# Chunk C of a batch in both partition halves, its matmuls on the two row halves of the array in turn, cosine and sine transforms in successive units

## The chip, the cores and the metric

The kernel runs on one core of one Trainium2 chip. The metric is the device time of one execution in microseconds (us). The kernel before takes 688.46 us, the median of three runs (687.03 to 688.67).

The engines are named as in the profile: PE is the matmul engine, PEld its weight loads, DVE the vector engine, ACT the scalar engine, POOL the GpSimd engine, SP the engine whose queue issues nearly all DMAs here.

## The reference

The input `x` is 8 batches of 3008 rows of 256 numbers. The first half of the work is the real part of a two-dimensional Fourier transform of each batch, the second half a gated feed-forward block on every row.

```python
X = np.fft.fft(x, axis=1)
X = np.fft.fft(X, axis=2)
y = X.real.reshape(24064, 256)
g = y @ w_gate                      # 256 x 1536
h = g / (1 + exp(-g)) * (y @ w_val)  # 256 x 1536
out = h @ w_out                     # 1536 x 256
```

Inputs and output are float32. The kernel multiplies in bfloat16 and accumulates in float32.

## The kernel before, in words

**The Fourier transform.** The transform over the 256 columns is folded into the weights once (`transform_w` makes `Wp`, `Wq` and `Wm` of `w_gate` and `w_val`). What is left for each batch is the transform over its 3008 rows. Its symmetries are used up to a fold by eight: rows are added and subtracted in groups (`fold_steps`, on POOL) until 188 folded positions remain, each with an odd-row and an even-row member (index `q` = 0, 1), and with 128 columns and a remainder. The 188 positions are kept in two chunks: chunk A has 128 of them, one on each partition, and chunk C has the other 60, on the lower 64 partitions for an even batch and on the upper 64 for an odd one. So a chunk-C tile holds two batches, and one fold of it serves a pair.

`fold_steps` gives seven steps for one `q`: sums and differences `SDf` (L153, twice), the even and the odd fold over the columns (L156, L157, L160), `Af` (L163), the coefficients `CE` (L166, L167) and `BB` (L170 to L172). `CE` serves the first half of a batch's output positions (`part` 0), `BB` the second (`part` 1). 

**The transform matmuls.** `transform(b, part, eos)` multiplies these coefficients (as weights, 128 columns wide) by tables of cosines and sines `Tab` (moving). `eo` 0 is the cosine transform and ends in tile `Pt`, `eo` 1 the sine transform and ends in `Qt`. For each `q` there is one accumulator: `q` 0 in a PSUM tile `v`, `q` 1 in a PSUM tile `g`. Into each go two matmuls of chunk A (128 rows of the array), then two of chunk C (64 rows). In `part` 0 the moving side has 189 or 188 columns, in `part` 1 it has 376. The sine transform of `part` 0 has a further group, `row0` (L543): weights of one single column, for chunk A and chunk C, which fill in row 0 of the result alone. When a `q` is done, ACT copies the `v` accumulator out (`od`, L575), and DVE adds and subtracts `od` and the `g` accumulator into the tiles `Pt` or `Qt` (L580). `whole_part` calls `transform` for `eo` 0 and then for `eo` 1, at once. Batch 0 is made at the start by a longer way, in which chunk C fills all 128 rows.

**The feed-forward block.** The 12032 columns of all batches' `Pt` and `Qt` are cut into 24 tiles of up to 512 columns; each column yields two output rows (position k and its mirror image). A unit is one tile and one of the 12 blocks of 128 hidden features; there are 288. In a unit, `part_a` makes the gate `g` and the value of the first output row, and `part_b`, one unit later, those of the mirror row. In the units where `split` holds (in most tiles blocks 0, 2, 3, 5, 7 and 9), the value product is taken apart into two accumulators `e` and `o`, both from the PSUM pool of the `v` tiles; DVE makes both values of them (`es` L731, then `vv` L733 and L735), and POOL multiplies them by the gates (L736, L758). In the other units DVE does the multiplication (L744, L762). ACT does the gate function (L728, L743, L757, L761). `OWork` multiplies the finished hidden tile of the tile before by `Wo` (L676), eight matmuls in each unit. Three units' worth fill a PSUM tile `o`, which ACT copies to one of four `ev` tiles (L682), and SP sends it out (L688, two or three DMAs).

**Order.** The order on each engine is the order of the program text (a manual schedule). The loop over units runs `run_loads` (three pending loads of `x`, issued on SP), `part_a`, output work, `part_b` of the unit before, output work, the fold steps that fall due (`fold_at`, `fold_step`), and the transform that falls due (`job_at`). The transforms of a batch stand in two units, nearly all of them in block 4 of a tile, of which the next block, 5, is a split one. Where a fold's first step falls due, all its loads that are still pending are issued at once. Chunk C of batches 2 and 3 is first folded in units 25 to 44; its loads follow in SP's queue on those of chunk A of batch 1. PSUM is divided into three `v` tiles, three `g` tiles and two `o` tiles; a new tile takes the buffer that has been free in program order for longest, and its first matmul waits until that buffer's last reader is done.

The chunk-C loads of one batch (`load_c`) are 15 transfers of four positions (L137: both rows of each, 2 KB runs), 4 transfers of 60 positions for the rows counted downwards (L139), and one for the middle row (L141).

Of the kernel before, what the change touches and what calls it, by code (L numbers as in the profile page):

```python
# [31 lines left out]
def kernel(  # L32
# [8 lines left out]
    nc = tc.nc  # L41
# [57 lines left out]
    XC = const.tile([P, 8, 2, D], F32, name="XC")  # L99
    SDf = const.tile([P, 2, 4, D], F32, name="SDf")  # L100
# [31 lines left out]
    def load_c(b, q):  # L132

        X3 = XC.rearrange("p a q d -> p a (q d)")
        p0 = 64 * (b % 2)
        pm = p0 + NCR
        return ([lambda h=h: q.dma_start(out=X3[p0 + LC * h:p0 + LC * (h + 1), 0:4, :],  # L137
                                         in_=up_block(b, JC - LC * h, LC)) for h in range(NC_)] +
                [lambda a=a: q.dma_start(out=X3[p0:p0 + NCR, 4 + a, :], in_=down_set(b, a, JC, LC, NC_))  # L139
                 for a in range(4)] +  # L140
                [lambda: q.dma_start(out=XC[pm:pm + 1, 0:4, 1],  # L141
                                     in_=rows_at(b, 0, [[R * D, 1], [R * D, 4], [1, D]]))])

    def fold_steps(eng, X, CE, BB, q, r, given=None):
# [4 lines left out]
        def sd(a, op):  # L152
            tt(SDf[r, a], X[r, 0:4, q, :], X[r, 7:3:-1, 1 - q, :], op=op)  # L153
# [11 lines left out]
        def ce():  # L165
            tt(CE[r, q, :, 0, :], Af[r, :, 0, :], Af[r, :, 1, :], op=Alu.add)  # L166
            tt(CE[r, q, :, 1, :], Af[r, :, 0, :], Af[r, :, 1, :], op=Alu.subtract)  # L167
# [10 lines left out]
    def coef_a(b):  # L178
        if b not in coefA:
            coefA[b] = (cp.tile([P, 2, 2, 2, P + 1], BF16, name="CEa"),  # L180
                        cp.tile([P, 2, 2, 2, P], BF16, name="BBa"))
        return coefA[b]

    def coef_c(b):
        p = b if b < 2 else 1 + b // 2
        if p not in coefC:
            coefC[p] = (cp.tile([P, 2, 2, 2, P + 1], BF16, name="CEc"),
                        cp.tile([P, 2, 2, 2, P], BF16, name="BBc"))
        return coefC[p]
# [32 lines left out]
    nc.vector.memset(XC0, 0.0)  # L222

# [175 lines left out]
    def heads(eng, ev, od, CE):  # L399

        eng.tensor_tensor(CE[:, :, 0, 0, P:P + 1], ev, od, op=Alu.add)
        eng.tensor_tensor(CE[:, :, 0, 1, P:P + 1], ev, od, op=Alu.subtract)
# [132 lines left out]
    def blocks(b, q):  # L535

        p0 = 64 * (b % 2)
        return [(0, slice(0, P), *coef_a(b)), (1, slice(p0, p0 + 64) if b else slice(0, P), *coef_c(b))]

    def row0(b, q, ps):  # L540
        for ch, r, CE, BB in blocks(b, q):
            for kind, cols in ((0, slice(0, GH + 1)), (1, slice(GH + 1, NCE))):
                nc.tensor.matmul(ps[0:1, cols], CE[r, q, 0, kind, P:P + 1], Tab[r, ch, q, 0, cols],  # L543
                                 start=False, stop=True, skip_group_check=True)

    def transform(b, part, eos, given=None):
        n = NCE if part == 0 else G
        ev, ods = {}, {}
        for q, pool, nm in ((0, psV, "v"), (1, psG, "g")):
            if given:  # L550
                ps = {eo: given[eo][q] for eo in eos}
                blk = []
            else:
                ps = {eo: pool.tile([P, T], F32, name=nm) for eo in eos}
                blk = blocks(b, q)
            for j, (ch, r, CE, BB) in enumerate(blk):
                tab = Tab[r, ch, q]
                for eo in eos:
                    for kind in range(2):
                        if part == 0:  # L560
                            cols = slice(0, GH + 1) if kind == 0 else slice(GH + 1, NCE)
                            l, r_ = CE[r, q, eo, kind, 0:P], tab[:, eo, cols]
                        else:
                            cols = slice(0, G)
                            l = BB[r, q, eo, kind, 0:P]
                            r_ = tab[:, (eo + kind) % 2, NOO:NTAB]
                        nc.tensor.matmul(ps[eo][:, cols], l, r_, start=(j == 0 and kind == 0),  # L567
                                         stop=(j == len(blk) - 1 and kind == 1), skip_group_check=True)
            if part == 0 and 1 in eos and not given:

                row0(b, q, ps[1])
            for eo in eos:
                if q == 0:
                    ods[eo] = odp.tile([P, NCE], F32, name="od")
                    nc.scalar.copy(ods[eo][:, 0:n], ps[eo][:, 0:n])  # L575
                else:
                    ev[eo] = ps[eo]
# [20 lines left out]
    def whole_part(b, part):  # L598
        transform(b, part, (0,))
        transform(b, part, (1,))  # L600

# [4 lines left out]
    for q in range(2):  # L606
        row0(0, q, acc[1][q])
# [165 lines left out]
    spread(("C", 1), 14, 6, 14)  # L773
# [10 lines left out]
    act_at = {}  # L784

# [5 lines left out]
    def fold_step(what, i, unit):  # L791
# [4 lines left out]
        if j == 0:  # L796
            if kind == "A":
                queue[what] = fold_steps(nc.gpsimd, XA, *coef_a(b), q, slice(0, P))
            else:
                queue[what] = fold_steps(nc.gpsimd, XC, *coef_c(b), q, slice(64 if b == 1 else 0, P))  # L800
        queue[what].pop(0)()
        if q == 1 and j == 1:
# [48 lines left out]
    for i, u in enumerate(units):  # L851
# [12 lines left out]
        run_loads(3)  # L864
# [14 lines left out]
        if i in job_at:  # L879
            whole_part(*job_at[i])  # L880
# [36 lines left out]
```

## Time and profile before

| what | value |
|---|---|
| median of three runs | 688.46 us |
| span of the profiled execution, first to last instruction | 685.5 us |
| the profiled execution's own time beside that span | not given; the median of the runs is 2.96 us above the span |
| PE busy | 672.8 us, 98% of the span |
| POOL busy | 579.1 us, 84% |
| DVE busy | 514.6 us, 75% |
| ACT busy | 432.9 us, 63% |
| transform matmuls (L567) | 256 |
| row 0 matmuls (L543) | 64 |
| granted PE clock | 1.0 throughout |
| DMA | 52.55 MB, mean 77 GB/s |

A row of the timeline has the start in us, the duration in us, the engine, the line of the kernel, the operation, the tiles as out<-in, the shape, and how many instructions were merged into the row. For a matmul, `64*128` says that the weights take 64 rows and 128 columns of the array. The end of a matmul is modelled and overlaps the next one's start, so distances are taken from start to start. A bracket at the end of a row gives the idle time of the engine before it and what ended that.

### The profile page before, as it was taken

Reading aid. Unit: us, or ns where it says so; the run is one execution under the profiler, and the core shown is the slowest. Engines: PE = TensorE matmul, PEld = TensorE weight load, DVE = VectorE, ACT = ScalarE, POOL = GpSimd, SP = SyncE. Lnnn points to the kernel's source line nnn. Section 1 sums busy time; section 2 is a strip of 40 time slices with the busy share of each in tenths; the row PEclk is TensorE's granted clock in tenths of the full one; section 3 lists DMA queues with packets and bytes.
Section 4 is the critical chain, followed back from the end, with each engine's and each line's share of the span. In section 5 each row is a group of like instructions: output and inputs, shape, how many; then the busy total and the mean of one; then the engine's idle time right before and its main releaser. Section 6 shows DMA issues by size and latency. Waiting matters only on the chain.

```text
span 685.5 us, 13259 instructions
## 1 busy us (share of the span) xinstructions
PE 672.8 (98%) x4374; PEld 414.2 (60%) x4374; DVE 514.6 (75%) x919; ACT 432.9 (63%) x764; POOL 579.1 (84%) x565
## 2 busy tenths in 40 slices
PE   8999999999999999999999999999999999999997
PEld 5446655666656566565665566655665656656676
DVE  8896667777777777777777777777786777788862
ACT  7676655666656666565666666655665656656663
POOL 8897987899998999999998989997999555658920
PEclk9999999999999999999999999999999999999999
DMA  9657353324315213335134111125111111101112
GB/s 220 115 77 133 102 138 113 96 76 101 99 32 134 67 51 105 86 71 131 41 76 116 48 32 47 47 58 128 46 48 32 38 40 33 47 31 47 47 48 70
DMA packets 45567, 52.55 MB, mean 77 GB/s; under 512 B 6290, under 2 KB 33466, under 8 KB 45498
## 3 DMA queue, kind: packets, MB, share of 16 engines
q1 hardware_dynamic: 42314, 49.35, 27.4%
q0 software_dynamic: 3184, 2.36, 2.7%
q8 instruction: 34, 0.56, 0.4%
q14 instruction: 35, 0.29, 0.2%
HBM read 29.39 MB, written 24.65 MB: 79 GB/s over the span
## 4 chain that ended last, share of the span: by engine, by line
PE 89%; DVE 5%; issue 2%; POOL 2%; ACT 0%; DVEq 0%; ACTq 0%; POOLq 0%
PE o L676 34%; PE v L716 17%; PE g L716 16%; PE g L753 9%; PE v L753 4%; PE g L567 3%; PE v L567 3%; DVE vv L735 3%; DVE vv L733 1%; PE v L543 1%; PE g L543 1%; PE g L856 1%; PE g L421 1%; PE v L421 1%; PE o L430 0%
## 5 line engine op out<-in xcount | busy, mean ns | idle before, releaser
L736 POOL TENSOR_TENSOR hp<-sgv,vv 128x512 bf16<-128x512 f32 (+1 forms) x126 | 160.1, 1272 | 54.3 <-DVE vv L733 42.4
L676 PE MATMUL o<-Wo,hp 128*128 128x256 bf16 (+2 forms) x1140 | 169.7, 273 | 0.0
L676 PE MATMUL o<-Wo,hm 128*128 128x256 bf16 (+2 forms) x1140 | 169.7, 273 | 0.0
L758 POOL TENSOR_TENSOR hm<-sgv,vv 128x512 bf16<-128x512 f32 (+1 forms) x126 | 159.6, 1272 | 8.5 <-ACT sgv L757 8.1
L676 PEld LDWEIGHTS <-hp 128*128 128x128 bf16 (+2 forms) x1140 | 111.9, 98 | 68.3 <-issue 7.8
L676 PEld LDWEIGHTS <-hm 128*128 128x128 bf16 (+2 forms) x1140 | 111.8, 98 | 64.8 <-issue 4.9
L744 DVE TENSOR_TENSOR hp<-sg,v 128x512 bf16<-128x512 f32 (+2 forms) x162 | 107.9, 666 | 33.2 <-ACT sg L743 32.4
L731 DVE SCALAR_TENSOR_TENSOR es<-bc,w,v 128x512 f32<-128x512 f32 (+1 forms) x126 | 93.7, 744 | 50.5 <-PE v L716 50.3
L762 DVE TENSOR_TENSOR hm<-sg,v 128x512 bf16<-128x512 f32 (+2 forms) x162 | 107.4, 663 | 24.1 <-ACT sg L761 14.4
L761 ACT ACTIVATE sg<-g 128x512 f32<-128x512 f32 (+2 forms) x162 | 94.7, 585 | 45.6 <-PE g L753 45.4
L743 ACT ACTIVATE sg<-g 128x512 f32<-128x512 f32 (+2 forms) x162 | 94.4, 583 | 45.0 <-PE g L716 43.5
L716 PE MATMUL g<-Qt,Wq 128*128 128x512 bf16 (+2 forms) x288 | 108.0, 375 | 0.5 <-DVE Qt L580 0.5
L716 PE MATMUL g<-Pt,Wp 128*128 128x512 bf16 (+2 forms) x288 | 108.1, 376 | 0.1
L716 PE MATMUL v<-Pt,Wp 128*128 128x512 bf16 (+2 forms) x288 | 108.0, 375 | 0.0
L753 PE MATMUL g<-Qt,Wm 128*128 128x512 bf16 (+2 forms) x288 | 108.0, 375 | 0.0
L757 ACT ACTIVATE sgv<-g 128x512 f32<-128x512 f32 (+1 forms) x126 | 75.3, 598 | 47.4 <-PE g L753 41.1
L728 ACT ACTIVATE sgv<-g 128x512 f32<-128x512 f32 (+1 forms) x126 | 75.1, 596 | 40.3 <-PE g L716 35.5
L733 DVE SCALAR_TENSOR_TENSOR vv<-v,es 128x512 f32<-128x512 f32 (+1 forms) x126 | 87.0, 690 | 17.6 <-PE v L753 1.0
L735 DVE SCALAR_TENSOR_TENSOR vv<-v,es 128x512 f32<-128x512 f32 (+1 forms) x126 | 85.7, 680 | 2.7 <-POOL hm L758 2.7
L716 PEld LDWEIGHTS <-Wp 128*128 128x128 bf16 x576 | 56.2, 98 | 41.0 <-issue 4.2
L682 ACT COPY ev<-o 128x512 f32<-128x512 f32 x90 | 52.7, 586 | 30.8 <-PE o L676 28.2
L153 POOL TENSOR_TENSOR SDf<-XA 128x1024 f32<-128x1024 f32 x28 | 66.0, 2364 | 5.2 <-DMA XC<-in_x_dram 3.3
(165 smaller groups left out, 738.0 us busy)
## 6 DMA issues: line engine op xcount, KB each, us to landing
out_dram<-ev SPq DMA_DIRECT2D x96, 128.0 KB
XA<-in_x_dram SPq DMA_DIRECT2D x32, 256.0 KB
XA<-in_x_dram SPq DMA_DIRECT2D x112, 64.0 KB
XC<-in_x_dram SPq DMA_DIRECT2D x32, 120.0 KB
XC<-in_x_dram SPq DMA_DIRECT2D x105, 32.0 KB
out_dram<-ev SPq DMA_DIRECT2D x12, 120.0 KB
out_dram<-ev SPq DMA_DIRECT2D x10, 112.0 KB
XA<-in_x_dram SPq DMA_DIRECT2D x1, 1024.0 KB
```

What stands on the lines that cost most here:

```text
L676: nc.tensor.matmul(ps[:n, j, :], hts[minus][:, f, c:c + n], Wo[:, f, :], start=(f == 0), stop=(f == nF - 1))
L716: nc.tensor.matmul(ps[:, :w], Wt[:, gv, fs], src[:, :w], start=start, stop=stop, skip_group_check=True)
L731: stt(es[:, :w], bc[t][:, :w], w0[:, f:f + 1], e[:, :w], op0=Alu.mult, op1=Alu.add)
L733: stt(vp[:, :w], o[:, :w], -0.5, es[:, :w], op0=Alu.mult, op1=Alu.add)
L735: stt(vm[:, w - 1::-1], o[:, :w], 0.5, es[:, :w], op0=Alu.mult, op1=Alu.add)
L736: nc.gpsimd.tensor_tensor(hts[t][0][:, f, :w], sg[:, :w], vp[:, :w], op=Alu.mult)
L743: nc.scalar.activation(sg[:, :w], g[:, :w], AF.Silu)
L744: nc.vector.tensor_tensor(hts[t][0][:, f, :w], sg[:, :w], v[:, :w], op=Alu.mult)
L753: nc.tensor.matmul(ps[:, :w], Wm[:, gv, f * P:(f + 1) * P], Qt[:, :w], start=False, stop=True, skip_group_check=True)
L758: nc.gpsimd.tensor_tensor(hts[t][1][:, f, :w], sg[:, :w], v[:, :w], op=Alu.mult)
L761: nc.scalar.activation(sg[:, :w], g[:, :w], AF.Silu)
L762: nc.vector.tensor_tensor(hts[t][1][:, f, w - 1::-1], sg[:, :w], v[:, :w], op=Alu.mult)
```

## The change

Chunk C of one batch is laid over both partition halves: the odd rows (`q` 0) on partitions 0 to 63, the even rows (`q` 1) on 64 to 127. Where the tile had the index `q`, it now has the batch of the pair. `load_c` therefore has two rounds of 15 and 4 transfers, with runs of 1 KB in place of 2 KB, and the middle row: 39 DMAs for a batch where there were 20. `run_loads` issues six at a time where chunk C is next. A fold of seven steps makes chunk C of one batch; batch 1, which stands alone, needs seven steps where it had fourteen on one half.

In `transform`, chunk A's matmuls of both accumulators come first, then chunk C's, which alternate between `q` 0 (rows 0 to 63 of the array, into `v`) and `q` 1 (rows 64 to 127, into `g`). The accumulators are read only after all of them. `row0` takes weights of 128 columns in place of one: `CE` gets a new layout in fixed tiles (`CEs`), in which the one wanted column is followed by 127 columns of zeros. Four POOL memsets at the very start write those zeros. `whole_part` is gone: the cosine transform of a part stands in its unit and the sine transform in the next one.

```diff
+    CEs = {(nm, i): const.tile([P, 2, 2, 3 * P + 1], BF16, name=f"CE{nm}{i}") for nm in "ac" for i in range(2)}
...
     def load_c(b, q):
...
+        bb = b % 2
+        steps = []
+        for qq in range(2):
+            p0 = 64 * qq
+            for h in range(NC_):
+                up = rows_at(b, 2 * (JC - LC * h) - 1 + qq, [[2 * D, LC], [R * D, 4], [1, D]])
+                steps.append(lambda p=p0 + LC * h, up=up: q.dma_start(out=XC[p:p + LC, 0:4, bb, :], in_=up))
+            for a in range(4):
+                down = rows_at(b, R * (a + 1) - 2 * JC + 1 - qq, [[2 * LC * D, NC_], [-2 * D, LC], [1, D]])
+                steps.append(lambda p=p0, a=a, down=down: q.dma_start(out=XC[p:p + NCR, 4 + a, bb, :], in_=down))
...
+    for CE in CEs.values():
+        nc.gpsimd.memset(CE[:, :, :, 2 * P + 2:3 * P + 1], 0.0)
...
+    def row0(CE, r, q, ch, qt, ps):
+        for kind, cols in KINDS:
+            nc.tensor.matmul(ps[:, cols], ce_zero(CE, r, q, kind), Tab[r, ch, qt, 0, cols],
+                             start=False, stop=True, skip_group_check=True)
...
+        if not given:
+            every = slice(0, P)
+            for eo in eos:
+                for q in range(2):
                     for kind in range(2):
+                        product(eo, kind, q, coef_a(b), every, q, 0, kind == 0)
+                    if part == 0 and eo == 1:
+                        row0(coef_a(b)[0], every, q, 0, q, ps[eo][q])
+            for eo in eos:
+                for kind in range(2):
+                    for q in range(2):
+                        if b == 0:
+                            product(eo, kind, q, coef_c(b), every, q, 1, False)
                         else:
+                            product(eo, kind, q, coef_c(b), half(q), b % 2, 1, False)
...
-    def whole_part(b, part):
-        transform(b, part, (0,))
-        transform(b, part, (1,))
...
-    spread(("C", 1), 14, 6, 14)
+    spread(("C", 1), 7, 6, 14)
...
         u = slot[jb]
-        while u in job_at:
-            u += 1
-        job_at[u] = jb
+        for eo in range(2):
+            while u in job_at:
+                u += 1
+            job_at[u] = (*jb, (eo,))
...
-        run_loads(3)
+        run_loads(3 if loads and loads[0][0][0] == "A" else 6)
...
         if i in job_at:
-            whole_part(*job_at[i])
+            transform(*job_at[i])
```

More of the change, by code (lines that the diff above doesn't have):

```diff
@@ L572, in transform @@
+        for q in range(2):
             for eo in eos:
@@ L606 @@
     for q in range(2):
-        row0(0, q, acc[1][q])
+        for ch, CE in ((0, CEa), (1, CEc)):
+            row0(CE, slice(0, P), q, ch, q, acc[1][q])
     unfolded(1, 1, SBc, False, True)
```

90 lines of the change are left out of this document (42 added, 48 removed).

## The prediction

> **What bounds the kernel now.** I read the page's busy times and its chain first:
>
> ```profile
> span 685.5 us, 13259 instructions
> PE 672.8 (98%) x4374; PEld 414.2 (60%) x4374; DVE 514.6 (75%) x919; ACT 432.9 (63%) x764; POOL 579.1 (84%) x565
> PE 89%; DVE 5%; issue 2%; POOL 2%; ACT 0%; DVEq 0%; ACTq 0%; POOLq 0%
> ```
>
> PE ends nearly every step, so time taken out of PE's stream counts, as long as the others keep up. POOL is the one to watch; the busy times by stretch (duration, then PE, PEld, DVE, ACT, POOL) say where:
>
> ```profile
> 110.00:220.00 110.00, 109.32 (x708) 66.86 (x706) 83.79 (x144) 69.05 (x124) 105.56 (x98) 1.00 0.31 84
> 220.00:330.00 110.00, 109.63 (x712) 66.51 (x711) 84.44 (x154) 69.64 (x122) 107.95 (x100) 1.00 0.31 85
> 330.00:440.00 110.00, 109.63 (x710) 67.33 (x708) 84.20 (x143) 70.19 (x123) 104.65 (x96) 1.00 0.23 60
> ```
>
> From 110 to 440 us POOL is idle for only 330 - 318.2 = 11.8 us.
>
> Then the timeline of PE, in a plain stretch, and over one `part` 0 and one `part` 1 of a batch (first and last rows), and the counts of chunk C's matmuls:
>
> ```profile
> 95.42 0.38 PE L716 MATMUL g<-Pt,Wp 128*128 128x512 bf16 x1
> 95.64 0.38 PE L716 MATMUL g<-Qt,Wq 128*128 128x512 bf16 x1
> ...
> 97.59 0.33 PE L567 MATMUL v<-Tab,CEa 128*128 128x189 bf16 x2
> 97.85 0.34 PE L567 MATMUL v<-Tab,CEc 64*128 64x189 bf16 x2
> ...
> 100.58 0.32 PE L543 MATMUL g<-Tab,CEc 64*1 64x189 bf16 x2
> 100.83 0.39 PE L716 MATMUL g<-Pt,Wp 128*128 128x512 bf16 x1
> ...
> 197.62 0.48 PE L567 MATMUL v<-Tab,BBa 128*128 128x376 bf16 x2
> 201.00 0.39 PE L716 MATMUL g<-Pt,Wp 128*128 128x512 bf16 x1
> ...
> L567 PEld LDWEIGHTS <-BBc x64: 91/95/98, 45.3 to 612.2; 64*128 64x128 bf16 x56, 128*128 128x128 bf16 x8
> L567 PEld LDWEIGHTS <-CEc x56: 92/95/98, 97.8 to 557.9; 64*128 64x128 bf16 x56
> ```
>
> A 512-column matmul takes 0.215 us from start to start (95.42 to 95.64), 0.42 ns a column. A pair of 189 and 188 columns should take 0.16 us and takes 0.26 (97.59 to 97.85). The extra comes wherever the shape of the weights changes (128 rows to 64, 128 columns to 1). `part` 0: 24 matmuls at 0.080 are 1.91 us, and 3.24 are taken (97.59 to 100.83); its 12 changes cost (3.24 - 1.91) / 12 = 0.11 us. `part` 1: 16 at 0.159 are 2.54, taken 3.38; 8 changes at 0.105. I use 0.105.
>
> **The change, part by part.**
>
> *Changes of shape.* Seven batches (the counts: 56 of each coefficient, 8 a batch) have 12 + 8 = 20 changes, 14.7 us. Afterwards a transform goes from chunk A to chunk C and back to the main work once; `row0` keeps 128 columns, so it adds none. Four transforms a batch make 8 changes, 5.9 us. Saved 8.8 us, and 0.2 in batch 0, whose single-column `row0` goes too. This is PE's own stream, nothing lies over it. The wider weights of `row0` load as chunk A's do, beside the matmul before; if that cover were gone, 56 loads of the 0.095 us in the rows above would cost 5 us.
>
> *Alternating halves.* Chunk C has a batch 8 + 4 matmuls of 0.080 and 8 of 0.159, 2.23 us; 15.6 us in seven batches. No row shows the two halves in turn. One end: one after the other, nothing gained. The other: two at a time, 7.8 us. Below nothing: each alternation counts as a change of shape; 3 + 7 + 3 + 3 = 16 a batch, 112 x 0.105 = 11.8 us lost. The nearest rows are the second matmuls of a 64-row pair, which pay nothing extra, and nothing that the rows show is shared by the two: other rows, other weights, other accumulators (`v` and `g`). I take overlap with 0.010 us over the ideal for each pair of matmuls, 10 pairs a batch: 7.0 us saved.
>
> The Trainium skill, "TensorEngine Tiling (Array Packing)", Key Properties, says that changing the tiling mode, "not just tile", drains the engine, and that different tiles load weights and multiply in parallel. By the first half the 0.105 us is that drain, and alternating halves pays none; by the second the sum has 7 us more than by the nearest rows taken strictly, one after the other. The trace agrees on the drain; no run here shows the parallel part yet.
>
> *Sine transform a unit later.* PE's work is only moved, but a wait comes in. The rows around the end of a transform pair and the next unit (PE, ACT, DVE), and the puts of a `part` 1:
>
> ```profile
> 172.37 0.39 PE L716 MATMUL g<-Pt,Wp 128*128 128x512 bf16 x1
> 174.54 0.38 PE L716 MATMUL g<-Pt,Wp 128*128 128x512 bf16 x1
> ...
> 171.42 0.47 ACT L575 COPY od<-v 128x377 f32<-128x377 f32 x1 [1.12 <-PE v L543]
> ...
> 172.54 1.27 DVE L580 TENSOR_TENSOR Qt<-g,od 128x188 bf16<-128x188 f32 x6 [0.84 <-PE g L543]
> 173.72 0.74 DVE L731 SCALAR_TENSOR_TENSOR es<-bc,w,v 128x512 f32<-128x512 f32 x1
> ...
> 199.48 1.07 DVE L580 TENSOR_TENSOR Pt<-g,od 128x272 bf16<-128x272 f32 x3 [1.86 <-PE g L567]
> ```
>
> So far `od` was copied while `g` was still being multiplied. Now both end together. With t the start of the next main matmul (172.37; DVE reacts at 172.54, 0.17 later), ACT copies from about t + 0.1 to t + 0.57, DVE puts from t + 0.6, `es` of block 5 starts 1.18 later (172.54 to 173.72) and ends at t + 2.5. The sine transform's turn is a unit later, t + 2.17 (172.37 to 174.54). Its `v` takes, by the order in which buffers come free, the one that `es` reads: PE waits about 0.4 us. In `part` 1 the puts are 0.2 shorter, the wait 0.2. Behind `es` on DVE stand the two `vv` and the mirror product of block 4, and ACT and POOL wait for those, but all of them are early enough for PE: the next unit's `v` takes the buffer that the second `vv` leaves at about t + 4.0, and is due at t + 4.3. The wait holds for 6 + 6 parts of batches 1 to 7, those that stand in blocks 4 and 5 with only 5 split (`part` 0 of batch 1 and `part` 1 of batch 0 stand in tiles without split units; the last part in one where 4 is split too, and the order gives it ACT's buffer): 3.6 us. Ends: 0 (DVE starts its puts sooner) and 12 x 0.74 = 8.9 (one more instruction like `es` ahead).
>
> *POOL.* A fold step costs the same on 64 and on 128 partitions (L153: 2.36 us in both forms), so pairs cost what they did, and batch 1 loses seven steps, some 11 us by the distance of 100.93 from 89.98. POOL then waits for chunk A's loads anyway, 3.3 us at 66.14, and those keep their place behind SP's outputs: worth nothing. The same 11 us cover the start of batch 1's fold, whose 39 loads land later than its 20 did.
>
> ```profile
> 66.14 4.68 POOL L153 TENSOR_TENSOR SDf<-XA 128x1024 f32<-128x1024 f32 x2 [3.32 <-DMA XC<-in_x_dram]
> 89.98 4.68 POOL L153 TENSOR_TENSOR SDf<-XC 128x1024 f32<-128x1024 f32 x2 [2.02 <-DMA XC<-in_x_dram]
> 100.93 2.35 POOL L153 TENSOR_TENSOR SDf<-XC 128x1024 f32<-128x1024 f32 x1
> 107.91 1.21 POOL L736 TENSOR_TENSOR hp<-sgv,vv 128x480 bf16<-128x480 f32 x1 [4.63 <-DVE vv L733]
> 121.74 1.20 POOL L736 TENSOR_TENSOR hp<-sgv,vv 128x480 bf16<-128x480 f32 x1 [2.27 <-DVE vv L733]
> ...
> 61.07 5.43 SPq L137 DMA_DIRECT2D XC<-in_x_dram  x9
> 87.81 0.64 SPq L141 DMA_DIRECT2D XC<-in_x_dram  x1
> ...
> L137 SPq DMA_DIRECT2D XC<-in_x_dram x105: 250/299/556, 9.9 to 281.2; - x105
> L139 SPq DMA_DIRECT2D XC<-in_x_dram x28: 833/850/942, 24.2 to 284.3; - x28
> ```
>
> SP's queue is where chunk C of batches 2 and 3 is late. Now 40 loads take from 61.07 to 88.4 us, of which 30 x 0.345 + 8 x 0.895 + 2 x 0.69 = 18.9 is issue (0.045 between two) and 8.5 outputs and waits. Then 78: 60 x 0.345 + 16 x 0.895 + 1.4 = 36.4, so the last is issued at 61 + 36.4 + 8.5 = 106 and landed at 107.5 (the fold at 89.98 began 1.5 us after the last issue). Batch 2's half, 18.2 us of issue, is there at about 87, in time; batch 3's first step, which POOL reaches at 100.93, starts at 107.5. Behind it on POOL waits the first split product, so far at 107.91 and, with PE some 1.5 us ahead by then, ready near 106.4: it comes at 109.9, 3.5 us late. POOL's next idle time, 2.27 at 121.74, absorbs part of that, less what PE is ahead: cost 2 us. If all that idle time were gone it would be 3.5. Later pairs are loaded long before their turn: six loads a unit are 6 x 0.345 = 2.1 us of SP in a unit of 2.17, and the four slow ones of each round (L139) make SP some us late, which four `ev` buffers bear. The bytes are the same, and the transfer engines have room (share 0.31 in the stretches above); the shorter runs cost nothing there. What is queued behind the loads on SP are the outputs; see the rival.
>
> ```profile
> DVE vv L735 <- POOL hm L758: 2.7, 3, 1.7
> ```
>
> Where DVE already waits for POOL (three places, in the waits list), block 5 now comes 2.4 us sooner after block 3, since the sine transform no longer stands between: 1 us each, 3 us. POOL in all 5 us; ends 0, and 9, the net gain of the eight parts between 110 and 440 us ((15.8 - 3.6) x 8/14 = 7) and the 2 above.
>
> *Start.* Four memsets of 4 x 127 numbers go ahead of POOL's first work.
>
> ```profile
> 1.82 0.19 POOL L250 MEMSET putC<- 128x128 f32 x1
> 3.93 1.16 POOL L302 TENSOR_SCALAR t<-kf,mM 128x377 int32<-128x377 f32 x2 [1.12 <-DVE mM L284]
> 5.89 1.83 POOL L302 TENSOR_SCALAR t<-kf,mM 128x377 int32<-128x377 f32 x2 [0.81 <-DVE mM L294]
> ```
>
> At 0.19 to 0.75 us each (as the row, or four times it) they take 0.8 to 3.0 us. POOL waits for DVE for 1.12 + 0.81 = 1.93 us in the rows behind; that hides all or leaves 1.1. I take 0.3, nearer to the row. If the wait for DVE grew with it, since DVE needs POOL's first column, the whole 3.0 would count.
>
> *Sum.* 685.5 - 8.8 - 0.2 - 7.0 + 3.6 + 5.0 + 0.3 = 678.4 us of span. The median of the runs shown stands 2.96 us above the span: **681.4 us**.
>
> **The rivals.**
>
> *Halves one after the other.* 7.0 less gained, and PE, less ahead, waits 2 us less for POOL: 686.4. For it: no row shows overlap. Against: nothing shared. Chance 0.14.
>
> *Alternation drains.* 681.4 + 7.0 + 11.8 - 4 (POOL no longer pressed) = 696.2. For it: a half is a different part of the array, as 64 rows are from 128. Against: the shape stays 64*128. It decides from 0.08 us per alternation. Chance 0.08.
>
> *SP's queue too late* (the slower side). Outputs from unit 27 on stand behind the 78 loads.
>
> ```profile
> 83.91 0.59 ACT L682 COPY ev<-o 128x512 f32<-128x512 f32 x1 [0.27 <-DMA XC<-in_x_dram]
> 90.78 1.15 SPq L688 DMA_DIRECT2D out_dram<-ev  x3
> 113.23 0.58 ACT L682 COPY ev<-o 128x512 f32<-128x512 f32 x1 [0.48 <-PE o L676]
> ...
> L141 SPq DMA_DIRECT2D XC<-in_x_dram x7: 637/639/650, 27.8 to 285.2; - x7
> ```
>
> The copy at 83.91 is sent at 90.78 now, near 109 then; the copy at 113.23, four later, needs its buffer. It decides from about 111. A strided target as in L141, 0.64 us against 0.30, would add 60 x 0.34 = 20 us of issue: ACT blocked 14 to 18 us, all behind it: 681.4 + 14 - 2 = 693.4. Against: L141 differs from L137 in having one partition too. Chance 0.16, smaller slips included.
>
> **How the numbers follow.** Forecast as summed 0.62. The range: best case overlap of 7.8, no wait, 1 for POOL, 685.5 - 9.0 - 7.8 + 1 + 2.96 = 672.7. The upper bounds of the two waits at once (8.9 and 9 in place of 3.6 and 5.0) give 681.4 + 9.3 = 690.7. I give 674 to 692, which leaves out the drain, the worst of SP and the last 1.3 us of the best case; the forecast's own range is 675 to 687. About 0.3% (2 us) is what a measurement of this kernel can tell from no change. Faster by more: 0.62 x 0.95 + 0.14 x 0.5 + 0.16 x 0.1 = 0.68; within: 0.62 x 0.04 + 0.14 x 0.35 + 0.16 x 0.15 = 0.10; slower 0.22.
>
> **What would show it.** Shape: between the last 128-row and the next main matmul a transform has two gaps of 0.1 us, not four to eight. Overlap: chunk C's pairs start a few ns apart, and a transform of `part` 1 takes 4 x 0.159 + 4 x 0.085 + 2 x 0.105 = 1.2 us, not 1.5. Wait: PE idle before chunk A's first `v` in block 5, ended by `es`. POOL: the fold at 100.93 moved to about 108, ended by a DMA. If SP's issue of L137's successor is near 0.6 us, or ACT waits for a DMA before `ev` after 105 us, or chunk C's pairs stand 0.19 apart, the prediction is wrong there.

## The result, and the profile after

The changed kernel takes 691.06 us (median of 15 runs, 688.43 to 692.70); the kernel before takes 688.50 us beside it (15 runs). The ratio is 1.0038, 95% interval 1.0027 to 1.0049: slower by 2.6 us, where 681.4 and faster had been forecast. The profiled run loses 9 us at one place in batch 3, 185 us into the span, that the prediction didn't name; the rest went much as forecast. The profiled run is the fastest of the 15 (688.43 us), and what the others lose besides stands in no trace. The time lies inside the stated range (674 to 692), but near an end that was added up from other waits.

The page of the changed kernel, its busy times:

```profile
span 686.7 us, 13388 instructions
PE 662.1 (96%) x4374; PEld 414.7 (60%) x4374; DVE 513.5 (75%) x919; ACT 432.4 (63%) x764; POOL 570.3 (83%) x558
```

The span is 1.2 us longer than before (686.7 against 685.5), and PE is busy for 10.7 us *less* (662.1 against 672.8). So PE's own work became shorter, and somewhere it waits instead. How much shorter is read further down, from the starts of the transforms' matmuls, since the busy time of a matmul rests on a modelled end and grows with a lower clock. The busy times by stretch (duration, then PE, PEld, DVE, ACT, POOL, the granted clock, the DMA engines' share, GB/s) say where:

```profile
110.00:220.00 110.00, 101.44 (x653) 62.41 (x652) 77.75 (x136) 63.22 (x114) 99.68 (x93) 0.97 0.36 99
...
184.00:190.00 6.00, 0.04 (x1) 0.00 (x0) 0.48 (x1) 0.48 (x1) 4.07 (x3) 0.91 0.22 74
190.00:196.00 6.00, 5.73 (x20) 2.67 (x20) 3.10 (x6) 2.39 (x5) 6.00 (x6) 0.52 0.00 0
```

From 110 to 220 us PE is busy for 101.44 us (before: 109.32), and its granted clock is 0.97. Inside it PE does next to nothing from 184 to 190 us (0.04 us), and from 190 to 196 its mean clock is 0.52.

The start of the main matmul of the same units in both kernels puts a price on that place. The timeline of PE, before, unit 73:

```profile
189.34 0.38 PE L716 MATMUL g<-Pt,Wp 128*128 128x512 bf16 x1
```

and after, unit 66 and unit 73:

```profile
173.19 0.39 PE L737 MATMUL g<-Pt,Wp 128*128 128x512 bf16 x1
...
197.07 0.38 PE L737 MATMUL g<-Pt,Wp 128*128 128x512 bf16 x1
```

Unit 66 started at 174.54 before (a row of the prediction), so here the changed kernel is 1.4 us ahead. At unit 73 it is 197.07 - 189.34 = 7.7 us behind. Some 9 us are lost within seven units. Without them the changed kernel would stand at about 691.06 - 9 = 682 us.

**Who waits for whom.** The waits of the changed kernel between 178 and 196 us (in total, times, longest), then the rows of POOL, DVE and PE:

```profile
POOL SDf L165 <- DMA out_dram<-ev: 10.0, 1, 10.0
...
PE v L737 <- DVE vv L756: 6.2, 1, 6.2
```

```profile
185.94 2.34 POOL L165 TENSOR_TENSOR SDf<-XA 128x1024 f32<-128x1024 f32 x1 [10.00 <-DMA out_dram<-ev]
188.23 1.26 POOL L779 TENSOR_TENSOR hm<-sgv,vv 128x512 bf16<-128x512 f32 x1
...
189.52 0.69 DVE L756 SCALAR_TENSOR_TENSOR vv<-v,es 128x512 f32<-128x512 f32 x1 [7.78 <-POOL hm L779]
...
190.27 0.59 PE L737 MATMUL v<-Pt,Wp 128*128 128x512 bf16 x1 [6.23 <-DVE vv L756]
```

POOL stands still for 10.00 us before the first step of the fold of batch 3's chunk A. The split product `hm` of the unit is queued behind that step on POOL and ends at 189.49. DVE's second `vv` and ACT's `sgv` need the buffer that it reads, PE's `v` needs the accumulator that `vv` reads, and it starts at 190.27, after 6.23 us of nothing. The granted clock fell within this gap: it is 0.96 from 188 to 189 us and 0.50 from 189 to 190, some 5 us after the start of PE's last matmul (183.66), and 1.00 again from 196 on. From its restart PE takes 197.07 - 190.27 = 6.8 us to the start of unit 73; before, the same work took 4.2 us (from 185.17). The lower clock is thus 2.6 us of the 9. The Trainium skill, "TensorE: Matmul & The Clock Gate", Why this matters for your kernels, names idle gaps of more than some 3 us as what halves the clock. The trace agrees: the clock was halved in this gap of 6.23 us.

What POOL waits for is told by SP's queue. The page's name for the releaser (`out_dram<-ev`) isn't the cause; the step reads `XA`, and `XA` comes late. The DMA queue of SP, after:

```profile
121.01 3.11 SPq L140 DMA_DIRECT2D XC<-in_x_dram  x6
...
163.53 0.64 SPq L145 DMA_DIRECT2D XC<-in_x_dram  x1
...
168.04 2.02 SPq L129 DMA_DIRECT2D XA<-in_x_dram  x6
...
177.79 3.28 SPq L131 DMA_DIRECT2D XA<-in_x_dram  x4
```

with POOL's last step that reads the old `XA`:

```profile
156.58 2.37 POOL L165 TENSOR_TENSOR SDf<-XA 128x1024 f32<-128x1024 f32 x1
```

and before, with POOL's steps that free and use `XA`:

```profile
144.52 0.65 SPq L141 DMA_DIRECT2D XC<-in_x_dram  x1
...
160.04 2.02 SPq L128 DMA_DIRECT2D XA<-in_x_dram  x6
```

```profile
157.65 2.37 POOL L153 TENSOR_TENSOR SDf<-XA 128x1024 f32<-128x1024 f32 x1
177.52 2.36 POOL L153 TENSOR_TENSOR SDf<-XA 128x1024 f32<-128x1024 f32 x1 [0.49 <-DMA XA<-in_x_dram]
```

Before, SP is through with the loads of batches 4 and 5 at 145.2 us and has time to spare. At 160.02 POOL ends the last step that reads the old `XA` (157.65 + 2.37), and the loads of batch 3's chunk A start at 160.04. After, 78 loads and the outputs between them hold SP from 121.01 to 164.17, nine outputs follow, and the same loads start at 168.04 although `XA` is free at 158.95 (156.58 + 2.37). The last is issued at 181.1 and POOL has its data at 185.94, 8.4 us later than at 177.52.

**What went as forecast.** PE over one cosine transform and one sine transform of `part` 1:

```profile
205.35 0.48 PE L572 MATMUL v<-Tab,BBa 128*128 128x376 bf16 x2
...
206.08 0.33 PE L572 MATMUL v<-Tab,BBc 64*128 64x376 bf16 x1
206.08 0.33 PE L572 MATMUL g<-Tab,BBc 64*128 64x376 bf16 x1
...
206.50 0.39 PE L737 MATMUL g<-Pt,Wp 128*128 128x512 bf16 x1
```

```profile
236.70 0.33 PE L572 MATMUL v<-Tab,CEa 128*128 128x189 bf16 x2 [0.30 <-DVE es L752]
...
237.89 0.39 PE L737 MATMUL g<-Pt,Wp 128*128 128x512 bf16 x1
```

Chunk C's matmuls start in pairs, at the same hundredth of a microsecond (206.08 and 206.08). The transform takes 206.50 - 205.35 = 1.15 us; the forecast said 1.2. Two gaps of 0.1 us are left, one ahead of chunk C and one behind it. The sine transform of a `part` 0 begins after 0.30 us of waiting for `es`; 0.4 was forecast.

### The profile page after: what moved, and what is told of

Read it like the earlier page. It is cut to its first block, busy times and chain, and to the rows that moved or that the text cites. A ratio compares the mean times of both kernels' runs of the same rounds, so it can differ in the third digit from the quotient of the medians.

```text
span 686.7 us, 13388 instructions
## 1 busy us (share of the span) xinstructions
PE 662.1 (96%) x4374; PEld 414.7 (60%) x4374; DVE 513.5 (75%) x919; ACT 432.4 (63%) x764; POOL 570.3 (83%) x558
## 3 DMA queue, kind: packets, MB, share of 16 engines
q0 software_dynamic: 3184, 2.36, 2.4%
## 4 chain that ended last, share of the span: by engine, by line
PE 80%; DVE 8%; POOL 4%; issue 4%; ACT 1%; DMA 1%; SPq 0%; DVEq 0%; ACTq 0%; POOLq 0%
PE o L697 31%; PE v L737 16%; PE g L737 15%; PE g L774 8%; PE v L774 4%; PE v L572 3%; DVE vv L756 2%; DVE Pt L604 1%; PE g L572 1%; POOL hm L779 1%; DVE es L752 1%; DMA out_dram<-ev 1%; DVE vv L754 1%; POOL SDf L165 1%; PE g L880 1%
## 5 line engine op out<-in xcount | busy, mean ns | idle before, releaser
L165 POOL TENSOR_TENSOR SDf<-XA 128x1024 f32<-128x1024 f32 x28 | 66.0, 2363 | 24.8 <-DMA XC<-in_x_dram 14.7
```

## The experiments

All ratios are against the kernel before, with 95% intervals. Two theories stood against each other at first. By the theory, the order of the loads on SP's queue makes the whole loss. By its main rival, the new transforms make it, spread over two units and pressing DVE, POOL or the accumulators.

**Chunk A's loads first.** The rate of chunk C's loads is halved, and chunk A's go to the head of the list, so that they pass what is left of chunk C's:

```diff
-                loads.extend((("A", b + 1), fn) for fn in load_a(b + 1, nc.sync))
+                loads[0 if b > 1 else len(loads):0 if b > 1 else len(loads)] = [
+                    (("A", b + 1), fn) for fn in load_a(b + 1, nc.sync)]
...
-        run_loads(3 if loads and loads[0][0][0] == "A" else 6)
+        run_loads(6 if loads and loads[0][0] == ("C", 2) else 3)
```

> The changed kernel, with one thing else: chunk C's loads of batches 4 to 7 go out three to a unit and chunk A's loads go ahead of them in the list, so that SP reaches batch 3's chunk A loads when POOL has freed XA (159 us), and not at 168.0. Theory (the whole loss is SP's order in units 71 to 73): the two steps of +8.2 and +0.8 us at units 72 and 73 go, POOL's fold of batch 3's chunk A starts at about 178 instead of 185.9, and the time is 691.1 - 9.0 = 682 us (680.5 to 683.5). Rival 1 (POOL is saturated in block 5 and the fold would be late anyway): 688 or more. Rival 2 (the stall only moves to batch 4's chunk C, whose last loads now go out after chunk A's): some later unit shows a step of several us, 685 or more.

Measured: 680.12 us, ratio 0.9892 (0.9876 to 0.9908). The timeline of POOL there, the same fold:

```profile
178.70 2.36 POOL L165 TENSOR_TENSOR SDf<-XA 128x1024 f32<-128x1024 f32 x1 [2.69 <-DMA out_dram<-ev]
```

SP issues the first of these loads at 160.98, 7 us sooner, POOL waits 2.69 us where it waited 10.00, and the step of 9 us at units 72 and 73 is gone from the starts of the units. Nothing but the rate and the order of the loads was touched. That place is the loss, and both rivals fall. The size is less exact: 680.12 lies just below the expected 680.5 to 683.5, and 10.9 us below the change as it was made, where 9.0 was expected. The two profiled runs differ by 8.3 us (688.43 and 680.17). Where the rest of the 10.9 lies stays open.

**Two loads a unit.** The same with two loads to a unit until unit 58:

```diff
-        run_loads(6 if loads and loads[0][0] == ("C", 2) else 3)
+        run_loads(6 if loads and loads[0][0] == ("C", 2) else
+                  3 if loads and loads[0][0][0] == "A" else 2 if 25 < i < 59 else 3)
```

> e1_a_first with the loads of batches 4 and 5 going out two to a unit until unit 58 in place of three. In e1_a_first SP still came to batch 3's chunk A only at 161.0 us, 2 us after XA was free (159.0), and POOL's fold waited 2.7 us. Theory (SP's lag sets that wait, in proportion): the first of these loads goes out at 159 to 160, POOL waits under 1.5 us, no step at units 72 and 73, and the time is e1_a_first's or up to 1 us less: 679 to 680.5 us. Rival (batch 4's chunk C, now fetched later, is what POOL waits for at units 87 to 105): a step there, 681 or more.

Measured: 679.43 us, 0.9878 (0.9865 to 0.9892), in the expected range. The first load goes out at 158.88, and POOL waits 1.78 us, a little more than the 1.5 expected. This kernel is the base of most of those below.

**The order alone.** Here the rates stay as the change has them. Only the 78 loads of each later round are held back until chunk A's are in the list:

```diff
+            loads.extend(held)
+            held.clear()
...
-                loads.extend((("C", b), fn) for fn in load_c(b, nc.sync) + load_c(b + 1, nc.sync))
+                (loads if b == 2 else held).extend(
+                    (("C", b), fn) for fn in load_c(b, nc.sync) + load_c(b + 1, nc.sync))
...
-    loads = []
+    loads, held = [], []
```

> The changed kernel with its rates of loads (six and three a unit) as they are; only the order differs: the 78 loads of batches 4 and 5 are held back until batch 3's chunk A loads are in the list, and stand behind them, and those of batches 6 and 7 behind batch 5's chunk A. Theory (order on SP's queue alone made the loss): SP issues nothing but outputs from 121 to 159 us, the first chunk A load goes out at 159 us, the moment XA is free, POOL's fold waits under 1 us, and the time is e6_two_a_unit's, 679.4 (678.5 to 681). Rival (the number of loads, or their bytes on the DMA engines, costs something of its own wherever they stand): 682 or more.

Measured: 679.01 us, 0.9875 (0.9860 to 0.9890). The timeline of SP's DMA queue in this kernel:

```profile
121.32 33.88 SPq L709 DMA_DIRECT2D out_dram<-ev  x25
160.53 2.02 SPq L129 DMA_DIRECT2D XA<-in_x_dram  x6
```

and of POOL, the step that frees `XA` and the next fold's first:

```profile
158.15 2.36 POOL L165 TENSOR_TENSOR SDf<-XA 128x1024 f32<-128x1024 f32 x1
177.71 2.37 POOL L165 TENSOR_TENSOR SDf<-XA 128x1024 f32<-128x1024 f32 x1 [0.20 <-DMA XC<-in_x_dram]
```

POOL frees `XA` at 158.15 + 2.36 = 160.51, the loads start at 160.53, and POOL waits 0.20 us. The same 78 loads, at the same rate, cost nothing when they stand behind the other twenty. It was the order.

**The loads alone, in the kernel before.** Its transforms stay, and each of chunk C's loads is cut in two:

```diff
-        return ([lambda h=h: q.dma_start(out=X3[p0 + LC * h:p0 + LC * (h + 1), 0:4, :],
-                                         in_=up_block(b, JC - LC * h, LC)) for h in range(NC_)] +
+        ups = [lambda h=h, s=s: q.dma_start(out=X3[p0 + LC * h:p0 + LC * (h + 1), 0:4, s * D:s * D + D],
+                                            in_=up_block(b, JC - LC * h, LC)[:, :, s * D:s * D + D])
+               for s in range(2) for h in range(NC_)]
...
-        run_loads(3)
+        run_loads(3 if loads and loads[0][0][0] == "A" else 6)
```

> The kernel before, with its transforms as they were; only each load of chunk C from batch 1 on is cut in two of half the bytes (39 for a batch in place of 20), six to a unit. Theory (the loads alone make the loss): SP issues the 78 loads of batches 4 and 5 until about 164 us, batch 3's chunk A loads start at about 168 in place of 160.0, POOL's fold waits some 10 us, and the time is 688.5 + 8 to 10 = 697 us (695 to 699). Rival (the loss comes of the transforms spread over two units, with their waits on VectorE, POOL or PSUM): 688.5, within 1 us.

Measured: 697.32 us, 1.0136 (1.0123 to 1.0149). The number is the expected one and the place is not. The timeline of POOL there, the fold of batches 2 and 3:

```profile
106.18 4.67 POOL L156 TENSOR_TENSOR SDf<-XC 128x1024 f32<-128x1024 f32 x2 [18.50 <-DMA XC<-in_x_dram]
```

The stall stands at batches 2 and 3, not at batch 3's chunk A. In this kernel both batches lie in one fold, one in each half of the partitions, so its first step needs all 78 loads, and SP issues the last at 104.6. POOL waits 18.50 us and PE loses 9.1 us at unit 41 and 1.8 us at unit 42. In the change the first half of the fold needs batch 2 alone. So this run shows that such loads without any new transform can cost 9 us by way of a fold that POOL reaches too early. It doesn't show batch 3's stall; the two runs above do.

**One half for both.** Now the transforms. Both halves' matmuls read rows 0 to 63:

```diff
-                            product(eo, kind, q, coef_c(b), half(q), b % 2, 1, False)
+                            product(eo, kind, q, coef_c(b), half(0), b % 2, 1, False)
...
-                            r = half(q)
+                            r = half(0)
```

> e6_two_a_unit with chunk C's matmuls of both halves reading rows 0 to 63: the same matmuls, shapes and order, but no two of them on different halves of the array. It leaves out the part of chunk C that rows 64 to 127 carry, from batch 1 on, and counts the other twice. Theory (the two halves really run at once, and this saved 7.4 us): e6 + 7.4 us (6.5 to 8.3). Rival (the records show the starts of a pair together, but PE hands them on one after the other): e6 within 1 us.

Measured: 682.42 us, 0.9924 (0.9911 to 0.9938): 3.0 us more than its base, where 7.4 was expected and a rival had less than 1. On PE the price is as expected; its timeline, chunk C of one cosine transform of `part` 1 and the next main matmul:

```profile
197.05 0.33 PE L572 MATMUL v<-Tab,BBc 64*128 64x376 bf16 x1
197.22 0.32 PE L572 MATMUL g<-Tab,BBc 64*128 64x376 bf16 x1
...
197.79 0.39 PE L737 MATMUL g<-Pt,Wp 128*128 128x512 bf16 x1
```

Matmuls on one half start 0.16 to 0.17 us apart, and from the first of chunk C to the next main matmul 0.74 us pass, against 0.42 with two halves (206.08 to 206.50). In `part` 0 it is 0.16 us more in the cosine and 0.32 us in the sine transform. Over seven batches that makes 7 x (0.32 + 0.32 + 0.16 + 0.32) = 7.8 us. The difference between that and 3.0 lies in PE's waits. Those of the base from 100 to 620 us:

```profile
PE v L572 <- DVE es L752: 1.7, 6, 0.3
PE g L737 <- ACT sgv L778: 1.5, 1, 1.5
PE g L572 <- ACT sgv L778: 0.7, 2, 0.5
PE g L572 <- POOL CEa L179: 0.7, 2, 0.3
```

and with one half:

```profile
PE v L572 <- DVE es L752: 1.3, 6, 0.2
PE g L572 <- POOL CEa L179: 0.3, 1, 0.3
PE g L572 <- ACT sgv L778: 0.2, 1, 0.2
```

A slower PE reaches these places later and waits 4.6 - 1.8 = 2.8 us less. (A fifth line of each list, `v` waiting for `vv`, stands at 0.4 and 0.5 us.) The lists count idle time alone. The starts of matmuls and units show some 4.3 us regained: 1.2 us at the sine transforms, which begin less late (0.08 us in `part` 0, 0.15 in `part` 1), 2.3 us at three cosine transforms (at 167, 277 and 306 us), and 0.8 us in units behind sine transforms. The spans of the two profiled runs differ by 3.2 us, so all but some 0.3 us is accounted for.

**Halves not in turn.** In the kernel with chunk A's loads first, two on one half, then two on the other:

```diff
-                for kind in range(2):
-                    for q in range(2):
+                for q in range(2):
+                    for kind in range(2):
...
-                    for kind, cols in KINDS:
-                        for q in range(2):
+                    for q in range(2):
+                        for kind, cols in KINDS:
```

> e1_a_first with chunk C's matmuls grouped by half: both kinds on rows 0 to 63, then both on rows 64 to 127, so that of each four matmuls one pair changes halves in place of two. Theory (matmuls on two row halves run at the same time, 75 ns gained at each transition within a run): half the gain of the transforms, 3.2 us, and about a quarter of row 0's 1.1 us go, so e1 + 3.5 = 685.5 us (684.5 to 686.5). Rival 1 (the halves take turns without running together, and what is gained is only fewer changes of shape): e1 within 0.5. Rival 2 (each change of halves costs something of its own): faster than e1 by 1 to 3.

Measured: 681.34 us, 0.9906 (0.9887 to 0.9924). Against 680.12 that is 1.2 us, with intervals that overlap; 3.5 was expected. Neither the theory nor a rival had what the timeline of PE shows, chunk C of a cosine transform of `part` 1:

```profile
200.94 0.33 PE L572 MATMUL v<-Tab,BBc 64*128 64x376 bf16 x1
200.94 0.33 PE L572 MATMUL g<-Tab,BBc 64*128 64x376 bf16 x1
201.10 0.32 PE L572 MATMUL v<-Tab,BBc 64*128 64x376 bf16 x1
201.11 0.32 PE L572 MATMUL g<-Tab,BBc 64*128 64x376 bf16 x1
```

The program's order is `v`, `v`, `g`, `g`. PE starts `v`, `g`, `v`, `g`: the third matmul, on the other half, starts at 200.94 beside the first, ahead of the second at 201.10. The overlap on PE is the same as with the halves in turn, to a few ns. The profiled run took 684.18 us, 4.0 us more than that of its base, and these lie elsewhere: 1.7 us at its start and 2.2 us at unit 72, where POOL's fold again waited (5.08 us).

**Half by half.** To see how far this goes, all of one half first, in the sine transform of `part` 0 four and four:

```diff
-                for kind in range(2):
-                    for q in range(2):
+                for q in range(2):
+                    for kind in range(2):
...
-                if part == 0 and eo == 1:
-                    for kind, cols in KINDS:
-                        for q in range(2):
+                    if part == 0 and eo == 1:
+                        for kind, cols in KINDS:
```

> e6_two_a_unit with all of one half's chunk C matmuls ahead of the other's: in the sine transform of part 0 four on rows 0 to 63 (two products, two of row 0) and then four on rows 64 to 127, elsewhere two and two as in e4_no_alternation. There the first matmul of the second half, third in the program, started 7 ns after the first and 79 ns ahead of the second. If each half takes its matmuls in its own order, whatever stands between them in the program: here the fifth starts some 10 to 15 ns after the first, all eight take 0.33 us as before, and the time is e6's, 679.4 (678.5 to 680.5). If only one matmul can be passed: the second half starts some 240 ns late in part 0's sine transform, 7 x 0.24 = 1.7 us more on PE, and up to that much at the end: 680 to 681.

Measured: 678.05 us, 0.9860 (0.9844 to 0.9877), a little below the expected range; against its base (0.9878) the intervals overlap. The timeline of PE, the first three starts of chunk C in a sine transform of `part` 0:

```profile
226.71 0.25 PE L572 MATMUL v<-Tab,CEc 64*128 64x189 bf16 x1
226.72 0.25 PE L572 MATMUL g<-Tab,CEc 64*128 64x189 bf16 x1
226.80 0.24 PE L572 MATMUL v<-Tab,CEc 64*128 64x188 bf16 x1
```

The fifth matmul of the program starts 0.01 us after the first and is ahead of the second. In these rows each half takes its matmuls in its own order.

**Row 0 with one column.**

```diff
-            nc.tensor.matmul(ps[:, cols], ce_zero(CE, r, q, kind), Tab[r, ch, qt, 0, cols],
+            nc.tensor.matmul(ps[0:1, cols], ce_zero(CE, r, q, kind)[:, 0:1], Tab[r, ch, qt, 0, cols],
...
-                            nc.tensor.matmul(ps[eo][q][:, cols], ce_zero(coef_c(b)[0], r, b % 2, kind),
+                            nc.tensor.matmul(ps[eo][q][0:1, cols], ce_zero(coef_c(b)[0], r, b % 2, kind)[:, 0:1],
```

> e6_two_a_unit with the weights of row 0's matmuls one column wide again, as in the kernel before (they then write row 0 alone, and add nothing to the others, as before). Theory (a change of the shape of the weights costs some 95 ns each): four changes more for each part 0, seven of them, and two to four more in batch 0: e6 + 2.8 us (2.4 to 3.3). Rival (zero-padded weights gain nothing): e6 within 0.7 us.

Measured: 680.38 us, 0.9892 (0.9878 to 0.9905), 0.95 us above its base, with intervals that overlap; 2.8 was expected, and less than 0.7 by the rival. The starts of the units show 0.38 us more at each of the seven `part` 0, 2.7 in all, four changes of 95 ns each. They also show 1.1 us given back at unit 113, where PE in the base waited 1.5 us for `sgv`, and 0.6 us at six other units. The price of a change of shape on PE stands; what arrives at the end is less.

**Both transforms in one unit.** The base is the kernel with chunk A's loads first:

```diff
-        for eo in range(2):
-            while u in job_at:
-                u += 1
-            job_at[u] = (*jb, (eo,))
+        while u in job_at:
+            u += 1
+        job_at[u] = jb
...
-            transform(*job_at[i])
+            transform(*job_at[i], (0,))
+            transform(*job_at[i], (1,))
```

> e1_a_first with cosine and sine transform of a part in one unit again, one behind the other. The prediction put the sine transform a unit later at 3.6 us of PE waiting for es: by that 682 - 3.6 = 678.4 us. Rival (the second unit costs nothing, because the same waits come with both in one unit, where the sine transform needs four accumulators within two units): 682 or above, up to 685.

Measured: 683.11 us, 0.9926 (0.9909 to 0.9942), 3.0 us slower. Of PE's waits from 100 to 620 us, the first:

```profile
PE g L737 <- DVE Pt L604: 7.6, 13, 0.7
```

PE waits for DVE's puts thirteen times, up to 0.7 us, 7.6 in all, before the next unit's `g`. With chunk C last, both accumulators of a transform end together, and two transforms in one unit hold two of the three `g` buffers until DVE's puts are done. The wait for `es` that the prediction priced is less than the wait it replaces.

**Two units apart.** The wait for `es` goes if the sine transform stands in block 6, which isn't split:

```diff
-            while u in job_at:
-                u += 1
-            job_at[u] = (*jb, (eo,))
+            job_at[u + 2 * eo] = (*jb, (eo,))
```

> e6_two_a_unit with the sine transform two units behind the cosine transform in place of one, so that it stands in a unit whose hidden block isn't split. In e1_a_first the first matmul of the sine transform came 0.46 us late in part 0 (seven times) and 0.20 us late in part 1 (six times), 4.3 us together, waiting for the accumulator that es reads. Theory (that wait goes, nothing takes its place): e6 - 3.9 = 676 us (675 to 677.5). Rival (the wait moves to the unit behind it): e6 within 1 us.

Measured: 677.75 us, 0.9853 (0.9838 to 0.9869), 1.7 us gained of 3.9, between what the theory and the rival expected. Of PE's waits from 100 to 620 us, the second:

```profile
PE g L878 <- DVE Qt L604: 1.4, 1, 1.4
```

The wait for `es` is gone from the list. This one came, at unit 36, where a sine transform ran into the first matmul of the next tile. That unit starts 2.9 us later than in the base, counted from the unit before; 1.2 us of this is the moved transform itself (unit 35 starts as much earlier), so some 1.6 us are lost there. The next kernel keeps two units only where the cosine transform stands in block 4:

```diff
-            job_at[u + 2 * eo] = (*jb, (eo,))
+            job_at[u + (2 if u % nF == 4 else 1) * eo] = (*jb, (eo,))
```

> e7_two_units_apart, but the two units lie between the transforms only where the first stands in block 4 of a tile; the sine transforms of batch 0's part 1 and batch 1's part 0, which there ran into the end of a tile (2.9 us late at unit 36, 1.6 us at units 12 and 13), stand one unit behind as in the change. Theory: e7's 677.75 less 2.5 to 3 us of what was lost there: 675 us (674 to 676.5). Rival (a delay at the end of a tile is made up by waits that it saves later): e7 within 1 us.

Measured: 676.31 us, 0.9837 (0.9820 to 0.9855), in the expected range, 11 us below the kernel before and the fastest here. Against e7 that is 1.4 us, not 2.5 to 3, with intervals that overlap: the expectation counted the moved transforms as lost. By the starts of the units 1.6 us come back at units 35 to 37 and 0.7 at units 11 to 13, and 1.25 are lost again at unit 65.

## Why the prediction was wrong

The failing step stands under *POOL*: "Later pairs are loaded long before their turn", and behind it "What is queued behind the loads on SP are the outputs". The first is true of the pairs, and the second leaves out that the loads of batch 3's chunk A are queued there too, and are due while the pairs aren't. The prediction worked out SP's issue for batches 2 and 3 (36.4 us for 78 loads) and not for batches 4 and 5. Its own numbers and the rows of before were enough for an estimate. It has the last load of batch 3's chunk C issued at 106. Behind that stand the 20 loads of batch 2's chunk A, whose first and last rows before are:

```profile
88.56 2.12 SPq L128 DMA_DIRECT2D XA<-in_x_dram  x6
...
100.14 3.46 SPq L130 DMA_DIRECT2D XA<-in_x_dram  x4
```

They take SP from 88.56 to 103.6, with the outputs between them, so until about 121 in the changed kernel. The 78 loads of batches 4 and 5 are 36.4 us more, until 157.4, and the ten outputs that stood between the loads of that round before, some 4 us, bring it to 161 or later, where 160.04 was needed. Measured are 121.01 for the first of the 78 and 164.17 for the end of the last. The rival *SP's queue too late* had the right queue and the wrong victim (the outputs and ACT). The strided target that it feared costs nothing: thirteen of these loads in a row take 4.58 us of SP, 0.35 each, as the prediction had it. Its victim shows up too, at the next round and small: a copy of ACT waits 3.19 us for its buffer, while SP sends the nine outputs that had queued up behind the loads of batches 4 and 5 (164.27 to 167.94). ACT waiting for a DMA before `ev` after 105 us is a sign of being wrong that the prediction itself had named.

```profile
167.56 0.58 ACT L703 COPY ev<-o 128x512 f32<-128x512 f32 x1 [3.19 <-DMA out_dram<-ev]
```

POOL's fold is what cost the time. The rival's 693.4 lies nearer to the result than the forecast, for a reason that it doesn't give.

The other steps, in order:

- *Changes of shape*, 8.8 us, and *Alternating halves*, 7.0 us: right on PE. By the starts of the matmuls a batch's transforms take 3.17 + 3.38 us before and 1.89 + 2.31 after (`part` 0 and 1), which is 16.4 us for seven batches, where 15.8 was forecast; 7.8 of that is the overlap. (The table of the kernel before counts 256 matmuls at L567; the trace has 240. No step rests on it.) Over both transforms `part` 1 takes 2 x 1.15 = 2.3 us where it took 3.38, and the sine transform of `part` 0 took 237.89 - 236.70 = 1.19. The ten chunk C pairs of a `part` 0 and a `part` 1 start together, as the forecast needed. Both were priced as if all of it reached the end; only the rival *Halves one after the other* took 2 us off for waits. The runs with one half and with one column give 3.0 of 7.8 and 0.95 of 2.7; nearly all of the rest are waits that a slower PE doesn't meet. The forecast had such waits as terms of their own, so its sum still held.
- *Sine transform a unit later*, 3.6 us (0.4 and 0.2 us each): 0.30 us of waiting, and with the restart behind it about 0.45 us late in `part` 0 and 0.20 in `part` 1, six times each, 3.9 us (the expectation above counts one `part` 0 too many). Right. What wasn't seen is that both transforms in one unit would have been 3 us slower still.
- *POOL*, 5 us. Batch 3's first step of chunk C starts at 106.83, forecast 107.5:

```profile
106.83 2.36 POOL L165 TENSOR_TENSOR SDf<-XC 128x1024 f32<-128x1024 f32 x1 [7.90 <-DMA XA<-in_x_dram]
```

  `hp` behind it comes at 109.15, forecast 109.9. The 2 us put down for it weren't lost; the units around it gain as much as elsewhere. The 3 us for POOL pressing are near to what the base shows (1.5 + 0.7 + 0.7 us in its waits), though PE waits there for `sgv` and `CEa`, and only 0.4 us for `vv`. So 2 us of this term weren't lost and the other 3 came out near by luck, from other waits.
- *Start*, 0.3 us: not to be told from the spread of the start, 24.8 to 26.5 us over the profiled runs.
- *The median above the span*, 2.96 us: every run on record lies 1.7 to 1.9 us above its own span (the change's profiled run 688.43 and 686.7). The 2.96 compares the median with the span of another run, so some 1.2 us of it are not part of any one run.

With the order mended the kernel takes 679.0 to 680.1 us, and the sum said 681.4. What the sum held comes out within 2.4 us; the term for twenty loads behind 78 was missing.

## What to carry to other kernels

When a change adds instructions to a queue that runs in program order, go through the queue to its end: list every later entry that the added ones delay, with the time at which each is due, and repeat the sum at each repetition of the loop, not only at the first. The entry that suffers may belong to another buffer and another engine than the one that was changed. Time taken from an engine that is busy for 98% of the span arrives at the end only as far as its neighbours keep up; here 3.0 of 7.8 us did.

## What wasn't expected of the hardware

TensorE started matmuls out of the program's order. With chunk C's matmuls grouped by half, the first on rows 64 to 127 started 7 ns (two matmuls ahead of it) or 14 ns (four ahead) after the first on rows 0 to 63, before the others of that half. Chunk C with the next restart took 0.45 us in a sine transform of `part` 0 with four ahead, against 0.44 with the halves in turn, and the kernel was no slower (678.05 and 679.43 us). Matmuls of one half stayed 0.08 us (189 columns) and 0.16 us (376 columns) apart. The Trainium skill, "TensorE: Matmul & The Clock Gate", The mechanism, has matmuls start and end strictly in order; these rows don't agree, for the start, between the two row halves. Their ends are modelled in the records, and nothing here shows them.
